# Third place for raw weight words, exponents by PSUM and remainders turned by VectorE, in a top-k attention with an FFN

## The chip, the cores and the metric

The kernel runs on one core of a Trainium2 chip. The metric is the device time of one execution in microseconds (us). Most executions of a kernel agree within 0.3%. A core has five engines with queues of their own: TensorE (PE, its weight loads shown as PEld), VectorE (DVE), ScalarE (ACT), GpSimd (POOL) and SyncE (SP, which only issues DMAs here). [...]

## The reference

Two blocks follow each other: attention that keeps the 32 largest scores of each row, and an FFN without bias.

```python
# q, k, v: (8 batches, 8 heads, 576 rows, 64) fp32
scores = scale * np.matmul(q, k.transpose(0, 1, 3, 2))
kth = np.partition(scores, -32, axis=-1)[..., -32:-31]
scores = np.where(scores >= kth, scores, -1e9)
attn = np.exp(scores - np.max(scores, axis=-1, keepdims=True))
attn = attn / (np.sum(attn, axis=-1, keepdims=True) + 1e-09)
x = heads_to_columns(np.matmul(attn, v))      # 4608 tokens x 512
h = x @ w_in                                  # 512 x 2048
return (h - np.tanh(h)) @ w_out               # 2048 x 512
```

The two weight matrices arrive in 64-bit floating point. The kernel reads their raw words and builds fp32 values itself.

## The kernel before

**Steps.** The attention is cut into 144 steps, 18 for each batch. A step takes a pair of heads (`hp`, four pairs) and 128 query rows of both (`qt`). 576 rows are four tiles of 128 and a remainder of 64; the remainders of two head pairs share one step (`J`, `rem`), two such steps a batch. In `plan()` (L530) the tiles of a batch are grouped into units of two tiles, which share FFN work. In batch 0 the first two tiles are units of one tile; in batch 7 the last two are. The remainders of two batches form a unit of their own (`rest`). A `Unit` has its FFN input `xT`.

**The loop.** The order of all engines is written out by hand (`manual_schedule`). Iteration n of the loop at L683 emits, in this order: `values` of an older step, `mask(n-1)`, `search(n)`, `scores(n+1)`, `expo(n-1)`, and the loads of later steps. `search` (L244) is VectorE's main work: four rounds of MAX8 (L271) and MATCH_REPLACE8 (L274) after two tensor operations on the scores (L263, L264). Between its rounds, `between(i)` places other VectorE work: the transposes of q and k rows (L218), the conversion of weights, and the turning of older weights.

**Turning the softmax weights.** The product with v needs the weights z with keys on partitions. There are two ways. With `pe=True`, `turn_pe` (L389) makes nine TensorE transposes into PSUM (L404) and three ScalarE copies (L407), and `values` follows two iterations after the step (`lag` 2). Otherwise `turn_z` (L365) lets VectorE transpose blocks of 32 x 32 (L372), `spread_keys` (L377) moves the blocks across partitions with 16 DMAs on SyncE's queue (L385), and `values` comes four iterations after the step. Before the change `pe` holds for batch 0, for the one-tile units of batch 7, and for all remainders. `zx2` are the two buffers of the second way, used in turn; the second one and `et_rem`, the turned weights of a remainder, lie in the tile `spare`.

**FFN.** A unit that is complete puts its FFN into the list `work`, in items of equal size: `ffn_h` (L471) computes h in the PSUM tiles `hps` (pool `h_ps`, two buffers) and then h - tanh(h); `ffn_o` (L497) the output product `ops`. `rate()` (L657) chooses how many items a step deals out, in four places of the iteration (`deal`). An item waits until the pieces of the weights that it needs are converted.

**Conversion of weights.** 32 pieces of 128 x 512 (16 of w_in, then 16 of w_out) are converted in iterations 0 to 10, two in each of the first two, three in each of the next eight, four in iteration 10 (`many`, L565). `convert` (L136) is a generator of three parts. It loads the raw words twice (L146, and L147 shifted by three bytes). Part 1 takes the exponent (L156 on VectorE, L157 and L158 on ScalarE) and the mantissa (L160, L163). Part 2 puts the sign to the exponent (L166, VectorE) and multiplies both (L169, GpSimd). `slots` (L128) are the places for raw words: two in `spare`, and one in each quarter of w_out until that quarter's own pieces come. The third entry of a slot is the piece from which it may not be used any more. A slot is loaded again when part 2 has run.

Of the kernel before, what the change touches and what calls it, by code (L numbers as in the profile page):

```python
# [8 lines left out]
AF = mybir.ActivationFunctionType  # L9
ALU = mybir.AluOpType  # L10
# [9 lines left out]
J = 4  # L20
# [28 lines left out]
def kernel(  # L49
# [25 lines left out]
    WJ = 4  # L75
# [34 lines left out]

    NW = 512


    spare = consts.tile([P, 4, NW, 2], U32, name="spare")
    later = spare[:].rearrange("p a n w -> p (a n w)").bitcast(FP32)
    zx2 = [consts.tile([P, 4 * S], FP32, name="zx")[:], later[:, 0 : 4 * S]]
# [8 lines left out]

    slots = [(spare[:, i], spare[:, 2 + i], 8 * CD) for i in range(2)]  # L128
    for j in reversed(range(WJ)):
        halves = [  # L130
            flat(w_out[j][:, 2 * i : 2 * i + 2, :]).bitcast(U32).rearrange("p (n w) -> p n w", w=2)
            for i in range(2)
        ]
        slots.append((*halves, (WJ + j) * CD))

    def convert(piece, slot):  # L136


        j, i = piece // CD, piece % CD
        if j < WJ:  # L140
            src, dst = moe_w_in[i * P : (i + 1) * P, j * NW : (j + 1) * NW], w_in[j][:, i, :]
        else:
            r0 = ((j - WJ) * FJ + i) * P
            src, dst = moe_w_out[r0 : r0 + P, :], w_out[j - WJ][:, i, :]
        raw, shifted, _ = slot
        nc.sync.dma_start(flat(raw), src.bitcast(U32))  # L146
        nc.sync.dma_start(  # L147
            flat(shifted).bitcast(U8)[:, 0 : 8 * NW - 4], src.bitcast(U8)[:, 3 : 8 * NW - 1]
        )
        yield  # L150
        hi = raw[:, :, 1]
        f = thpool.tile([P, NW], FP32, tag="th", name="f")
        fu = f[:].bitcast(U32)


        nc.vector.tensor_scalar(fu, hi, 20, 0x7FF, ALU.logical_shift_right, ALU.bitwise_and)  # L156
        nc.scalar.activation(f[:], fu, AF.Relu, bias=e1151[:], scale=-(2.0**23))  # L157
        nc.scalar.activation(f[:].bitcast(I32), f[:], AF.Relu, bias=e255[:], scale=-1.0)  # L158

        nc.vector.tensor_scalar(  # L160
            dst.bitcast(U32), shifted[:, :, 0], 0x0FFFFFFF, None, ALU.bitwise_and
        )
        nc.scalar.activation(dst, dst.bitcast(U32), AF.Copy, bias=1.0, scale=2.0**-28)  # L163
        yield

        nc.vector.scalar_tensor_tensor(  # L166
            out=fu, in0=hi, scalar=0x80000000, in1=fu, op0=ALU.bitwise_and, op1=ALU.bitwise_or
        )
        nc.gpsimd.tensor_tensor(dst, dst, f[:], ALU.mult)  # L169
        yield  # L170
# [15 lines left out]
    def load_rows(name, b, hp, exact):  # L186

        if b == 0 and hp and not exact:
            x = early[2 * hp - 2 + (name == "q")]
        else:  # L190
            x = ldpool.tile([P, S], FP32, tag=f"{name}in", name=f"{name}in")[:]
        raw[name, b, hp] = x
        src = {"k": k, "q": q}[name]
        for a in range(NG):
            h, d = 2 * hp + a // 2, a % 2 * G
            nc.sync.dma_start(  # L196
                x[a * G : (a + 1) * G, :].rearrange("i (n d) -> i n d", d=G),
                src[b, h, :, d : d + G].rearrange("(n i) d -> i n d", i=G),
            )
# [177 lines left out]
    def spread_keys(n):  # L377


        zx = zxs.pop(n)  # L380
        et = ets[n] = etpool.tile([P, 4 * S], FP32, tag="et", name="et")
        w = steps[n].nq * S // 2
        for a in range(NG):
            for c in range(NG):
                nc.sync.dma_start(  # L385
                    et[group(c), a * w : (a + 1) * w], zx[group(a), c * w : (c + 1) * w]
                )
# [142 lines left out]
    def plan():  # L530
        steps.clear(), done.clear()

        def block(b, qt):
            return [(slice(0, P), out[b * S + qt * P : b * S + (qt + 1) * P, :])]

        rest = None
        for b in range(B):
            if b % 2 == 0:
                rest = Unit(
                    [[(half(i), out[(b + i) * S + JP : (b + i + 1) * S, :]) for i in range(2)]], "xTr"  # L540
                )

            parts = [(0, 1), (2, 3)]
            if b == 0:
                parts[0:1] = [(0,), (1,)]
            if b == B - 1:
                parts[1:2] = [(2,), (3,)]
            for a, qts in enumerate(parts):
                unit = Unit([block(b, qt) for qt in qts], "xT")
                pe = b == 0 or len(qts) == 1  # L550
                for hp in range(NHP):
                    for i, qt in enumerate(qts):
                        steps.append(Step(b, hp, qt, unit, 0, i, len(qts), pe))
                    if hp == NHP - 1:
                        done[len(steps) - 1] = unit
                    if hp % 2 and a == (0 if b == B - 1 else len(parts) - 1):
                        steps.append(Step(b, hp - 1, J, rest, b % 2 * R, pe=True))
                        if hp == NHP - 1 and b % 2:
                            done[len(steps) - 1] = rest
        for g, after in zip(steps, steps[1:]):  # L560
            if after.pe and not after.rem and not g.pe:
                g.lag = 3
# [4 lines left out]
    def run(exact):  # L567
# [4 lines left out]
        def at(n, fn):  # L572
            todo.setdefault(n, []).append(fn)
# [26 lines left out]
        def load_piece():  # L600
            k = len(loaded)
            usable = [x for x in free if x[2] > k]
            if k < pieces and usable:
                free.remove(usable[0])
                piece = convert(k, usable[0])
                next(piece)
                loaded.append((piece, usable[0]))

        def part(x, k):
            next(loaded[k][0])  # L610
# [5 lines left out]
        for _ in slots[NHP:]:  # L616
            at(-4, load_piece)
        started = 0
        for m in range(max(many) + 1 if pieces else 0):
            mine = range(started, min(started + many[m], pieces))  # L620
            started = mine.stop
            seq = [(1, k) for k in mine[:1]]
            for k in mine[1:]:
                seq += [(1, k), (2, k - 1)]
            seq += [(2, k) for k in mine[-1:]]
            for i, x in enumerate(seq):
                at_round.setdefault((m, 3 * i // max(len(seq) - 1, 1)), []).append(
                    lambda x=x: part(*x)
                )
# [27 lines left out]
        def rate():  # L657


            have, low, high = len(work), 0.0, None  # L660
            coming = sorted((t, u.n // 8) for u, t in ready.items() if t > n)
            for t, k in coming + [(NS + 4, 0)]:
                r = have / max(t - n, 1)
                high = r if high is None else min(high, r)
                have += k
            for u, t in begun.items():
                if t > n and u in before:
                    need = [i + 1 for i, x in enumerate(work) if x[1] is before[u]]
                    if need:
                        low = max(low, need[-1] / (t - n))  # L670
            return max(low, high)
# [3 lines left out]
        def deal(part):  # L675
            nonlocal credit
            credit += part * share
            while work and credit > 0 and work[0][0] <= converted[0]:
                work.pop(0)[2]()
                credit -= 1  # L680
            credit = min(credit, 1.0)

        for n in range(-4, NS + 4):  # L683
            pe = here(-2) and steps[n - 2].pe
            if here(-3) and not steps[n - 3].pe:
                spread(n - 3)
            for m in (n - 4, n - 3):
                if 0 <= m < NS and steps[m].last and steps[m].lag == n - m:
                    values(m)
            share = rate()  # L690
            if pe:
                w = turn_pe(n - 2)
                next(w)
            if here(-1):
                mask(n - 1, exact)
            if here(0):
                search(n, exact, between)
            elif here(-2):
                between(0)
            if here(-2) and not pe and steps[n - 2].last:  # L700
                spread_keys(n - 2)
            if pe:
                spread(n - 2)
            deal(0.4)
            if here(1):
                scores(n + 1)
            if pe:
                next(w)
            if here(-1):
                expo(n - 1)  # L710
            deal(0.2)
            if pe and steps[n - 2].last:
                values(n - 2)
            deal(0.2)
            for fn in todo.pop(n, []):
                fn()
            deal(0.2)
# [48 lines left out]
```

## Time and profile before

| | |
|---|---|
| time, 3 runs | 1573.74 us median, 1572.37 to 1576.3 |
| profiled span | 1571.8 us, mean granted TensorE clock 0.977 |
| TensorE busy | 1463.9 us (93%) |
| VectorE busy | 1322.7 us (84%) |
| ScalarE, GpSimd busy | 907.7 and 945.5 us |
| FFN matmuls (L481 and L502) | 476.0 and 524.7 us busy |
| transposes on TensorE (L404) | 360 records, 62.3 us busy |
| conversion L166 | 32 records: 17 with the mean 1165 ns, 15 with 933 ns |
| spread DMAs (L385) | 832 issues |

The page has sums over the span; the 40 slices below it, each 39 us long, show how they are spread. A group of instructions has its busy time, the mean of one in ns, and the idle time of its engine just before it with what ended it. The chain of waits is the sequence of work that ended last, followed back from the end. As matmuls are pipelined and their ends are modelled, TensorE's busy time has to be held against counts of records.

### The profile page before, as it was taken

Reading aid. Unit: us, or ns where it says so; the run is one execution under the profiler, and the core shown is the slowest. Engines: PE = TensorE matmul, PEld = TensorE weight load, DVE = VectorE, ACT = ScalarE, POOL = GpSimd, SP = SyncE. Lnnn points to the kernel's source line nnn. Section 1 sums busy time; section 2 is a strip of 40 time slices with the busy share of each in tenths; the row PEclk is TensorE's granted clock in tenths of the full one; section 3 lists DMA queues with packets and bytes.
Section 4 is the critical chain, followed back from the end, with each engine's and each line's share of the span. In section 5 each row is a group of like instructions: output and inputs, shape, how many; then the busy total and the mean of one; then the engine's idle time right before and its main releaser. Section 6 shows DMA issues by size and latency. Waiting matters only on the chain.

```text
span 1571.8 us, 25605 instructions
## 1 busy us (share of the span) xinstructions
PE 1463.9 (93%) x7834; PEld 940.6 (60%) x7834; DVE 1322.7 (84%) x3810; ACT 907.7 (58%) x1637; POOL 945.5 (60%) x1533
## 2 busy tenths in 40 slices
PE   2566699899999999999999999999999999999998
PEld 1355376556566565656666565656666666666675
DVE  7987689999999999998999999998999899874300
ACT  4877577556556565656556565656555565654431
POOL 2777467657567575657467575756566565644521
PEclk9877799999999999999999999999999999999999
DMA  9844112333532334233432343333432334210000
GB/s 248 297 172 168 69 30 56 88 86 65 115 88 61 90 82 91 69 80 75 100 88 62 84 94 83 74 79 76 97 92 61 82 84 96 55 45 7 8 8 16
DMA packets 245009, 134.43 MB, mean 86 GB/s; under 512 B 205440, under 2 KB 205440, under 8 KB 244864
## 3 DMA queue, kind: packets, MB, share of 16 engines
q1 hardware_dynamic: 244864, 132.71, 34.7%
q8 instruction: 64, 1.05, 0.3%
q14 instruction: 81, 0.66, 0.1%
HBM read 61.85 MB, written 9.44 MB: 45 GB/s over the span
## 4 chain that ended last, share of the span: by engine, by line
PE 81%; DVE 8%; ACT 4%; SPq 3%; POOL 2%; DMA 1%; issue 1%; DVEq 0%; ACTq 0%; POOLq 0%
PE hps L481 29%; PE ops L502 29%; PE av L428 9%; PE scps L233 9%; PE zt L404 2%; DVE m L271 2%; DVE ab L274 2%; PE av L436 2%; SPq L196 1%; SPq L385 1%; DVE f L166 1%; ACT z L303 1%; DMA spare<-in_moe_w_out_dram 1%; ACT sc L241 1%; ACT f L157 1%
## 5 line engine op out<-in xcount | busy, mean ns | idle before, releaser
L502 PE MATMUL ops<-w_out,g 128*128 128x512 f32 x1152 | 524.7, 599 | 0.0
L481 PE MATMUL hps<-xT,w_in 128*128 128x256 f32 (+1 forms) x2304 | 476.0, 362 | 0.2 <-POOL xT L452 0.2
L271 DVE MAX8 m<-ab 128x8 f32<-128x288 f32 (+1 forms) x1152 | 464.9, 445 | 0.0
L306 POOL TENSOR_TENSOR z<-sc,z 128x576 f32<-128x576 f32 x288 | 400.0, 1411 | 106.3 <-ACT z L303 106.3
L481 PEld LDWEIGHTS hps<-xT,w_in 128*128 128x128 f32 x2304 | 399.2, 195 | 63.5 <-issue 14.4
L274 DVE MATCH_REPLACE8 ab<-m,ab 128x288 f32<-128x288 f32 x864 | 376.2, 443 | 0.0
L502 PEld LDWEIGHTS ops<-w_out,g 128*128 128x128 f32 x1152 | 210.9, 192 | 232.0 <-issue 229.7
L303 ACT ACTIVATE z<-sc,tb 128x576 f32<-128x576 f32 x288 | 207.8, 770 | 138.3 <-POOL tb L290 138.3
L495 POOL TENSOR_TENSOR g<-g,th 128x512 f32<-128x512 f32 x144 | 183.8, 1276 | 130.2 <-ACT g L494 126.3
L241 ACT COPY sc<-scps 128x1152 f32<-128x1152 f32 x144 | 160.9, 1117 | 121.5 <-PE scps L233 117.0
L326 ACT ACTIVATE z<-z,nb 128x576 f32<-128x576 f32 x288 | 221.7, 775 | 5.3 <-POOL z L306 5.2
L263 DVE TENSOR_TENSOR ab<-scps,sc 128x576 f32<-128x576 f32 x144 | 107.0, 743 | 133.2 <-POOL bad L310 73.3
L233 PE MATMUL scps<-kT,qT 64*128 64x288 f32 (+1 forms) x1280 | 185.5, 439 | 31.0 <-DVE qT L218 28.8
L233 PEld LDWEIGHTS scps<-kT,qT 64*128 64x128 f32 (+1 forms) x1280 | 100.5, 181 | 122.3 <-issue 65.5
L428 PE MATMUL av<-et,vb 128*64 128x256 f32 (+1 forms) x1152 | 133.5, 368 | 39.9 <-ACT et L407 34.2
L493 ACT ACTIVATE th<-hps 128x512 f32<-128x512 f32 x144 | 85.3, 592 | 114.7 <-PE hps L481 107.1
L452 POOL TENSOR_TENSOR xT<-xs 128x256 f32<-128x256 f32 (+1 forms) x72 | 48.0, 667 | 157.2 <-ACT xs L440 157.0
L428 PEld LDWEIGHTS av<-et,vb 128*64 128x64 f32 x1152 | 77.6, 140 | 100.2 <-ACT et L407 37.8
L440 ACT COPY xs<-av 128x512 f32<-128x512 f32 (+1 forms) x88 | 44.7, 508 | 154.9 <-PE av L436 154.8
L336 POOL TENSOR_SCALAR rd<-den 128x2 f32<-128x2 f32 x144 | 33.4, 232 | 146.7 <-ACT z L326 113.1
L266 DVE MAX8 ab<-ab 128x8 f32<-128x288 f32 x288 | 116.4, 445 | 0.0
L264 DVE TENSOR_TENSOR ab<-scps,sc 128x576 f32<-128x576 f32 x144 | 107.4, 746 | 0.0
(59 smaller groups left out, 1319.0 us busy)
## 6 DMA issues: line engine op xcount, KB each, us to landing
et<-spare SPq DMA_DIRECT2D x416, 72.0 KB, 2.0
et<-zx SPq DMA_DIRECT2D x416, 72.0 KB, 2.0
kin<-in_k_dram SPq DMA_DIRECT2D x116, 72.0 KB, 2.4
qin<-in_q_dram SPq DMA_DIRECT2D x116, 72.0 KB, 2.5
vb<-in_v_dram SPq DMA_DIRECT2D x64, 128.0 KB, 2.5
out_dram<-ot SPq DMA_DIRECT2D x32, 256.0 KB, 2.2
spare<-in_moe_w_out_dram SPq DMA_DIRECT2D x11, 512.0 KB, 4.2
spare<-in_moe_w_out_dram SPq DMA_DIRECT2D x11, 511.5 KB, 5.1
```

Source lines behind the costliest of these rows:

```text
L233: nc.tensor.matmul(ps[rows, t, s, 0:S2], qT[g.b, g.hp + i][half(t), qs], kT[g.b, g.hp + i][half(t), ks], start=True, stop=True,)
L241: nc.scalar.copy(sc[:], ps[:, :, :, 0:S2])
L266: nc.vector.max(ab[:, t, S2 : S2 + 8], lo[:, t, :])
L271: nc.vector.max(m[:, t, m8], last[t] if i == rounds - 1 else cur[t])
L274: nc.vector.match_replace(nxt[t], m[:, t, m8], cur[t], NEG)
L303: nc.scalar.activation(zv[:, t, :], scf[:, t, :], AF.Relu, bias=tb[:, t : t + 1], scale=-BIG)
L306: nc.gpsimd.tensor_tensor(zv[:, t, :], scf[:, t, :], zv[:, t, :], ALU.subtract)
L326: nc.scalar.activation(x["zv"][:, t, :], x["zv"][:, t, :], AF.Exp, bias=x["nb"][:, t : t + 1], scale=scale, accum_out=den[:, t : t + 1],)
L428: nc.tensor.matmul(av[half(t), 0, cols], vb[g.b, hp][:, t, c, :] if c < J else vr[g.b, hp][:, t, :], es[:, :, (J + 1) * t + c if c < J els ...
L481: nc.tensor.matmul(cur[u][:, s : s + w], w_in[j][:, c, fo : fo + P], u.xT[:, c, 0:w], start=(c == 0), stop=(c == CD - 1),)
L495: nc.gpsimd.tensor_tensor(g, g, th[:], ALU.subtract)
L502: nc.tensor.matmul(cur[u][:], u.g[o // 1024][:, o % 1024 // 512, o % 512 : o % 512 + P], w_out[f // FJ][:, f % FJ, :], start=(f == 0), sto ...
```

## The change

It has five parts.

1. A third place for raw words that lasts for all 32 pieces, in the first `zx2` buffer, which no step uses before batch 1. The slot that expires first is now taken first.
2. For the pieces of w_in, the exponent goes from ScalarE to VectorE through a PSUM tile of the pool `h_ps` and no more through SBUF.
3. Three of the four DMAs that load the first q rows are issued on ScalarE's queue. Part 1 of the first piece runs before the first search.
4. Only batch 0 turns its weights by TensorE. The remainders of the batches 1 to 7 and the last two tiles of batch 7 take the second way; these two tiles are one unit again.
5. `deal` counts the pieces that were converted before the iteration began, so that no FFN item is placed ahead of a conversion of the same iteration. In the order of TensorE's instructions nothing moves by this up to step 31.

```diff
+    first = zx2[0][:, 0 : 4 * NW].bitcast(U32).rearrange("p (a n w) -> p a n w", a=2, w=2)
     slots = [(spare[:, i], spare[:, 2 + i], 8 * CD) for i in range(2)]
+    slots.append((first[:, 0], first[:, 1], 8 * CD))
...
-        nc.scalar.activation(f[:].bitcast(I32), f[:], AF.Relu, bias=e255[:], scale=-1.0)
+        e = h_ps.tile([P, NW], FP32, tag="h", name="e")[:] if j < WJ else f[:]
+        nc.scalar.activation(e.bitcast(I32), f[:], AF.Relu, bias=e255[:], scale=-1.0)
...
-            out=fu, in0=hi, scalar=0x80000000, in1=fu, op0=ALU.bitwise_and, op1=ALU.bitwise_or
+            out=fu, in0=hi, scalar=0x80000000, in1=e.bitcast(U32), op0=ALU.bitwise_and, op1=ALU.bitwise_or
...
-            nc.sync.dma_start(
+            queue = nc.scalar if a and (name, b, hp, exact) == ("q", 0, 0, False) else nc.sync
+            queue.dma_start(
...
-        et = ets[n] = etpool.tile([P, 4 * S], FP32, tag="et", name="et")
+        rem = steps[n].rem
+        et = ets[n] = et_rem if rem else etpool.tile([P, 4 * S], FP32, tag="et", name="et")
...
-            if b == B - 1:
-                parts[1:2] = [(2,), (3,)]
...
-                pe = b == 0 or len(qts) == 1
+                pe = b == 0
...
-                        steps.append(Step(b, hp - 1, J, rest, b % 2 * R, pe=True))
+                        steps.append(Step(b, hp - 1, J, rest, b % 2 * R, pe=pe))
...
-                free.remove(usable[0])
-                piece = convert(k, usable[0])
+                slot = min(usable, key=lambda x: x[2])
+                free.remove(slot)
+                piece = convert(k, slot)
...
+        if pieces:
+            at(-1, lambda: part(1, 0))
...
+            seq = [x for x in seq if x != (1, 0)]
...
-            while work and credit > 0 and work[0][0] <= converted[0]:
+            while work and credit > 0 and work[0][0] <= usable:
...
-            share = rate()
+            share, usable = rate(), converted[0]
```

More of the change, by code (lines that the diff above doesn't have):

```diff
@@ L603, in load_piece @@
             if k < pieces and usable:
-                free.remove(usable[0])
-                piece = convert(k, usable[0])
+                slot = min(usable, key=lambda x: x[2])
+                free.remove(slot)
+                piece = convert(k, slot)
                 next(piece)
-                loaded.append((piece, usable[0]))
+                loaded.append((piece, slot))
         def part(x, k):
```

## The prediction

> **What bounds the kernel now.** I read the page's busy line and slices first.
>
> ```profile
> PE 1463.9 (93%) x7834; PEld 940.6 (60%) x7834; DVE 1322.7 (84%) x3810; ACT 907.7 (58%) x1637; POOL 945.5 (60%) x1533
> PE   2566699899999999999999999999999999999998
> DVE  7987689999999999998999999998999899874300
> ```
>
> There are three stages: about 200 us (five slices of 39 us) in which TensorE is half idle, a long middle in which TensorE and VectorE are both full, and a tail from about 1390 us in which VectorE runs out of work. The busy times of each stretch say it in us:
>
> ```profile
> 60.00:80.00 20.00, 8.86 (x47) 6.22 (x48) 19.37 (x50) 16.32 (x32) 15.47 (x20) 0.62 0.67 226
> 160.00:180.00 20.00, 7.35 (x27) 3.36 (x25) 8.45 (x22) 10.80 (x17) 7.20 (x7) 0.76 0.30 105
> 600.00:800.00 200.00, 200.00 (x1023) 124.59 (x1023) 184.19 (x529) 117.26 (x209) 127.70 (x212) 1.00 0.38 84
> ```
>
> (After the length: busy us of PE, PEld, DVE, ACT, POOL, then granted clock, DMA share, GB/s.) A busy PE may be a waiting PE, so I counted. The chain of waits repeats itself from 779.07 to 1129.53 us: 36 steps in 350.5 us. Prices from dense runs: the last unit, and one steady step.
>
> ```profile
> 1536.69 14.29 PE hps L481 x128
> 1550.98 13.75 PE ops L502 x32
> ...
> 711.64 1.04 PE L404 MATMUL zt<-ident,z 128*128 128x128 f32 x8
> 712.40 3.32 PEld L481 LDWEIGHTS hps<-xT,w_in 128*128 128x128 f32 x16
> 712.51 3.62 PE L481 MATMUL hps<-xT,w_in 128*128 128x256 f32 x16
> ```
>
> An hps record of 128 columns takes 14.29/128 = 0.112 us (0.222 at 256), an ops record 13.75/32 = 0.430. One item of the FFN (8 hps records at 256 columns, or 4 ops records) is thus about 1.75 us. The program deals 4 items a step: 144 x 1.75 = 252.0. Scores: 32 x 1.2 + 4 x 2.4 = 48.0. Values of a pair of tiles with rx (from 700.77 to 703.36 in the timeline) 2.6 x 16 = 41.4; of a remainder (719.22 to 720.70) 1.48 x 4 = 5.9. Nine transposes zt of a remainder: the next hps starts 0.87 us after the first eight and about 0.15 us after the ninth, so 1.02 x 4 = 4.1. Sum 351.4 against 350.5: the middle is TensorE work without holes. VectorE, at 92%, is next.
>
> The start is another regime. One VectorE line there has two prices:
>
> ```profile
> 61.79 0.67 DVE L166 SCALAR_TENSOR_TENSOR f<-w_out,f 128x512 uint32<-128x512 uint32 x1
> 62.59 1.27 POOL L169 TENSOR_TENSOR w_in<-w_in,f 128x512 f32<-128x512 f32 x1 [0.92 <-ACT w_in L163]
> 63.13 1.28 DVE L166 SCALAR_TENSOR_TENSOR f<-w_out,f 128x512 uint32<-128x512 uint32 x1
> ...
> 170.44 0.43 DVE L156 TENSOR_SCALAR f<-spare 128x512 uint32<-128x512 uint32 x1 [3.30 <-DMA spare<-in_moe_w_out_dram]
> 176.78 0.43 DVE L156 TENSOR_SCALAR f<-spare 128x512 uint32<-128x512 uint32 x1 [2.55 <-DMA spare<-in_moe_w_out_dram]
> ```
>
> The third line overlaps the POOL product above it and takes twice as long. The last two are VectorE waiting for raw words in step 10, which lasts 27.05 us (L263 at 153.8 to 180.8) where its neighbours last 16 to 17.
>
> [...] L166 takes 0.67 to 0.69 us alone and 1.27 to 1.36 us where a POOL tensor operation runs, while L263 and L264, with one PSUM operand, average 743 and 746 ns. [...] Here the DMA share is 0.98 in the first 20 us, so I expect little.
>
> **The change part by part.**
>
> *First q rows on ScalarE's queue.* The eight issues of the first k and q rows run from 0.72 to 4.90 us, and qT starts at 7.44 when the last row lands. Three issues (1.6 us) go to a queue idle until 10.6 us. Bound: 0 to 1.6; with the DMA engines full I take 0.9. Everything behind on SyncE's queue also moves up, raw words included.
>
> *First half of piece 0 moved before step 0.* L156 and L160 (0.39 + 0.42 us) move into VectorE's idle 3.54 us before L263 at 11.76. Worth 0.8.
>
> *Exponents by PSUM, 16 pieces.* Of the 16 w_in pieces, 9 L166 took 1.27 to 1.35; each falls to 0.68. ScalarE's L158 writes PSUM instead (0.72 us either way, I assume). The two h_ps buffers are free: the first hps comes in step 6, when the last w_in piece is done. In steps 0 to 2 VectorE is full, but the raw words land just in time (piece 3 made L160 wait 0.60 us until 32.32), so I replayed these steps, with the durations of the timeline, against landings 1 us earlier. L263 starts at 10.9 instead of 11.8; VectorE reaches L160 of piece 1 at 16.3 and waits for its words until 17.3 (18.34 before); step 1 starts at 23.0 instead of 23.8. L160 of piece 3 waits until 31.3; step 2 starts at 35.3 instead of 36.8. Pieces 4 to 6 land ahead, the third L166 (1.30 before) saves 0.6 more: step 3 starts at 48.7 to 48.8 instead of 50.9. That is 2.2 us for the three edits together. In steps 3 to 5 (13.4 us each) both long L166 lie on the loop f L158, L166, search, L166, POOL L169, rx, zt, et: 0.67 + 0.61, less about 0.1 where the exponential of L326 ends last: 1.2 a step, 3.6.
>
> *Third place for raw words.* Step 10 loses its waits except for piece 31, requested only when piece 28 is done. Replayed: L166 of piece 28 ends at 165.6 as before, piece 30 follows at once, piece 31 lands about 172, the step ends near 174.7 instead of 180.8: 6.1. Steps 6 to 9 wait for ScalarE and TensorE, not for words: nothing.
>
> Start together: 2.2 + 3.6 + 6.1 = 12. It is kept: steps 11 to 137 get the same number of FFN items as before.
>
> *Remainders of batches 1 to 7 turned by VectorE and DMA.* 14 steps lose 1.02 us of TensorE (and 1.36 of ScalarE, hidden) and gain a 1.36 us transpose on VectorE and 16 DMA issues. In batch 1 VectorE is the limit (no idle time from step 34 to 42); the first remainder's transpose fits into the 2.38 us wait of step 33, the second costs 1.25, so nothing in sum. In batches 2 to 7, 12 x 1.02 = 12.2, if VectorE fits: 92% becomes about 95%. The new wait: `values` of the remainder, at the head of TensorE's order, waits for those DMAs, and all scores and FFN matmuls queue behind it. SyncE's issues take 0.61 us each, 10 us for sixteen; behind the spread of the pair before and eight k and q loads, the remainder's last part lands some 0.5 to 1.5 us before its `values`. I take 2 us lost in all, 0 to 3.5 for each as bounds. So 10.
>
> *Last eight steps.* 8 x 1.02 = 8.2 us of transposes go. Values at 128 columns cost as much as 20 x 0.089 (14 in 1.24 us at 57.46) + 0.15 = 1.92 a step; two make 3.84 against 2.6 for a pair: 4 x 1.24 = 5.0. FFN work is the same 82 items from step 138 on, with 12 more of them behind the last scores; TensorE stays full, since 5 items a step make 11.7 us against VectorE's 9.5. At the end no old FFN work is left between the last values and the last unit's hps: xs and xT, 0.59 + 0.73 + handovers, expose 2.0. Net 11.2.
>
> Sum: 12 + 10 + 11.2 = 33; 1573.7 - 33 = **1540**.
>
> **Rivals.**
> - *Loads gate the start.* The DMA share of 1.08 from 20 to 40 us speaks for it, the free landings from piece 4 on (5 us ahead or more) against. The start gives 1 instead of 12: 1551.
> - *VectorE's gaps come back too.* After each TensorE remainder L263 waits 2.4 to 3.2 us. If that is a true stall, some 1.2 us more for each of 12 goes: 1540 - 14 = 1526. Against it stands the sum of 351.4.
> - *The DMA path is late.* At the upper bound of 3.5 us for every remainder TensorE waits 14 x 3.5 = 49 us on top of the 12 + 12.2 + 11.2 gained: 1574 - 35 + 49 = 1588, slower. For it: two spreads in consecutive steps fill SyncE's queue. Against it: landings of pairs in the trace are 4 us ahead of their use.
>
> **How the numbers follow.** Forecast 0.58, gated start 0.20, returned gaps 0.12, late DMA 0.10, of which 0.06 with a partial loss that still ends at or under 1574 and 0.04 slower. The range, 1526 to 1556, reaches both nearer rivals and leaves out the late DMA. Faster by over 0.3% 0.93 (0.03 of the partial losses end within 0.3%), same 0.03, slower 0.04.
>
> **What would show it.** L166 of the w_in pieces near 0.69 whatever POOL does; step 10 near 21 us; zt gone after batch 0; 36 steps of the middle in 346 to 347 us; a tail of 64 ops records. Wrong if TensorE waits on DMA at the remainder's av, or if VectorE has no idle time in the middle.

## The result and the profile after

The changed kernel takes 1548.53 us (median, 1546.23 to 1550.22) against 1573.05 us for the kernel before on the same chip: a ratio of 0.9839, 95% interval 0.9818 to 0.9861. It was run once more later, on the chip of the last experiments: 1549.55 us against 1574.24, ratio 0.9839 (0.9826 to 0.9853). The gain is 24.5 us; the forecast was 33.

The busy line and the rows of slices of TensorE and VectorE, from the page of the changed kernel:

```profile
PE 1440.6 (93%) x7428; PEld 912.4 (59%) x7428; DVE 1347.3 (87%) x3828; ACT 883.4 (57%) x1567; POOL 941.5 (61%) x1525
PE   2467899999999999999999999999999999999997
DVE  6997889999999999999999999999999999997300
```

406 TensorE records have gone. VectorE is busy 25 us longer and now stays full to the 36th of the 40 slices. The three stretches shown of the kernel before, in the view of busy times by stretch:

```profile
60.00:80.00 20.00, 11.02 (x57) 7.90 (x59) 19.13 (x56) 17.92 (x35) 14.79 (x23) 0.66 0.93 346
160.00:180.00 20.00, 12.53 (x59) 6.31 (x58) 18.23 (x52) 13.98 (x26) 11.03 (x17) 0.74 0.15 53
600.00:800.00 200.00, 199.69 (x991) 127.71 (x990) 190.31 (x541) 118.72 (x210) 131.01 (x214) 1.00 0.41 91
```

From 160 to 180 us VectorE is busy 18.2 us (8.5 before): most of the wait in step 10 is gone. From 600 to 800 us VectorE is at 95%, as forecast, and TensorE has its first holes, 0.3 us in 200.

To see where the time came from, I compared the starts of L267 (L263 before), the first VectorE instruction of every step, up to the last `ops` record. All figures are profiled us; the second column of the changed kernel is its second profile (the experiment `again`).

| stretch | before | after | after, again | gain | forecast |
|---|---|---|---|---|---|
| start to step 3 | 50.9 | 51.0 | 49.1 | -0.1, 1.8 | 2.2 |
| steps 3 to 5 | 40.1 | 37.1 | 37.1 | 3.0 | 3.6 |
| steps 6 to 9 | 62.7 | 60.9 | 61.5 | 1.9, 1.2 | 0 |
| step 10 | 27.1 | 20.6 | 19.7 | 6.5, 7.3 | 6.1 |
| steps 11 and 12 | 16.1 | 17.5 | 17.4 | -1.4, -1.3 | 0 |
| steps 13 to 45, batch 1 for the most part | 299.3 | 301.4 | 302.2 | -2.1, -2.9 | 0 |
| steps 46 to 137 | 895.6 | 887.0 | 887.9 | 8.6, 7.8 | 10 |
| step 138 to the start of the last ops record | 172.3 | 162.1 | 162.1 | 10.2 | 11.2 |
| from there to the end | 7.7 | 10.8 | 10.8 | -3.1 | 0 |
| span | 1571.8 | 1548.3 | 1547.7 | 23.5, 24.1 | 33 |

The groups of the first 100 us show what PSUM did. This is the view of groups by line and shape, for VectorE (count, busy us, mean ns, idle before):

```profile
L169 DVE SCALAR_TENSOR_TENSOR f<-w_out,e 128x512 uint32<-128x512 uint32 x10 | 6.7, 675 | 0.7 <-ACT e L161 0.6
L169 DVE SCALAR_TENSOR_TENSOR f<-w_out,f 128x512 uint32<-128x512 uint32 x2 | 2.1, 1052 | 0.1
L169 DVE SCALAR_TENSOR_TENSOR f<-zx,e 128x512 uint32<-128x512 uint32 x2 | 1.3, 674 | 0.2 <-ACT e L161 0.2
```

In all sixteen pieces with e from PSUM the instruction takes 0.66 to 0.69 us, also in the eight that run under a GpSimd tensor operation from start to end. With f from SBUF, as in the pieces of w_out, the two shown take 1.05 us in the mean; over all sixteen such pieces it is 0.67 to 0.69 us without a GpSimd tensor operation beside it (six) and 1.27 to 1.43 with one (ten). The last lines of the chain of waits:

```profile
1468.94 14.28 issue
1483.26 0.73 POOL xT L457
1484.03 26.60 PE hps L486 x122
1510.63 27.48 PE ops L507 x64
1538.19 0.59 ACT ot L517
```

The tail is the forecast one: one unit of two tiles, 64 ops records, straight behind the last xT.

Two more stages are compared in groups by line and shape, for TensorE. From step 46 to step 137, two lines before and one after:

```profile
L481 PE MATMUL hps<-xTr,w_in 128*128 128x128 f32 x256 | 30.0, 277 | 0.0
L404 PE MATMUL zt<-ident,z 128*128 128x128 f32 x108 | 16.4, 279 | 0.0
L486 PE MATMUL hps<-xTr,w_in 128*128 128x128 f32 x384 | 45.4, 277 | 0.0
```

From step 138 to the last ops record, three lines before and two after:

```profile
L404 PE MATMUL zt<-ident,z 128*128 128x128 f32 x72 | 11.0, 277 | 0.3 <-ACT xs L440 0.3
L428 PE MATMUL av<-et,vb 128*64 128x128 f32 x128 | 8.8, 279 | 0.0
L428 PE MATMUL av<-et,vr 128*64 128x128 f32 x32 | 3.1, 273 | 0.0
L433 PE MATMUL av<-et,vb 128*64 128x256 f32 x80 | 9.7, 385 | 0.0
L433 PE MATMUL av<-et,vr 128*64 128x256 f32 x20 | 3.0, 379 | 0.0
```

All transposes zt are gone from both stages: 108 are nine for each of the twelve remainders of batches 2 to 7, 72 are nine for each of the last eight steps.

### The profile page after: what moved, and what is told of

It is laid out like the page before. It is cut to its first block, busy times and chain, and to the rows that moved or that the text cites. A ratio compares the mean times of both kernels' runs of the same rounds, so it can differ in the third digit from the quotient of the medians.

```text
span 1548.3 us, 25298 instructions
## 1 busy us (share of the span) xinstructions
PE 1440.6 (93%) x7428; PEld 912.4 (59%) x7428; DVE 1347.3 (87%) x3828; ACT 883.4 (57%) x1567; POOL 941.5 (61%) x1525
## 4 chain that ended last, share of the span: by engine, by line
PE 73%; DVE 9%; SPq 5%; ACT 4%; DMA 3%; issue 3%; POOL 2%; DVEq 0%; ACTq 0%; POOLq 0%
PE hps L486 27%; PE ops L507 27%; PE av L433 9%; PE scps L237 8%; SPq L390 4%; DVE ab L278 3%; DVE m L275 3%; PE av L441 2%; SPq L200 1%; DMA zx<-in_moe_w_in_dram 1%; DVE spare L376 1%; DVE ab L270 1%; DVE ab L267 1%; DVE ab L268 1%; ACT sc L245 1%
## 5 line engine op out<-in xcount | busy, mean ns | idle before, releaser
L486 PEld LDWEIGHTS hps<-xT,w_in 128*128 128x128 f32 x2176 | 392.4, 193 | 73.4 <-issue 24.4
L267 DVE TENSOR_TENSOR ab<-scps,sc 128x576 f32<-128x576 f32 x144 | 107.6, 747 | 70.1 <-POOL bad L314 58.2
```

What stands on the lines that cost most here:

```text
L486: nc.tensor.matmul(cur[u][:, s : s + w], w_in[j][:, c, fo : fo + P], u.xT[:, c, 0:w], start=(c == 0), stop=(c == CD - 1),)
```

## The experiments

All times below are medians of four or five runs, with the kernel before at 1573.61, 1572.83 and 1574.24 us in the three groups, each on a chip of its own. Runs of one kernel lie up to 5.0 us apart, so effects of 2 us are read from the traces.

**one_queue.** All first q rows on SyncE's queue.

```diff
-            queue = nc.scalar if a and (name, b, hp, exact) == ("q", 0, 0, False) else nc.sync
+            queue = nc.sync
```

> The changed kernel with all first q rows back on SyncE's queue; the rest as changed. In the changed kernel 10.3 us pass from the last ops record to the end of the span, 3.1 more than in the kernel before, and SyncE's last DRAIN lasts 2.2 us (0.06 before). Theory: the second hardware DMA queue has to be drained at the end; without it the DRAIN is below 0.3 us and the time from the last ops record to the end is 7 to 8 us. The start loses at most 1 us by the later q rows, since the DMA engines are full there. Sum: 1.5 to 2.5 us faster than the changed kernel, about 1546.5. Rival A: the end has nothing to do with the queue (another length of the last stores); DRAIN stays at 2.2 us, the time is 1548.5 to 1550. Rival B: the two queues are worth 2 us at the start; then 1550 or more even if the end gets shorter.

Measured: 1551.07 us, ratio 0.9855 (0.9840 to 0.9870). The theory fell. The pause at the end stays, 2.2 us, only at another instruction of SyncE's list: it now lies three instructions earlier, at a semaphore wait and not at the DRAIN, just as many as the three issues that were put into the list. The last ops record starts 10.7 us before the end, as before this edit. And in this one profile the second queue is worth more than I thought. Step 0 starts at 12.5 us, in the kernels with two queues at 10.3 to 11.2. Part of this is the new place of part 1 of piece 0: VectorE stands at its L163 for the second copy until 12.15 us, while ScalarE's copy of the scores, for which the first search waits, has ended at 11.31. What was to save 0.8 us delays the first search by 1.2 us here, and by 0.5 in `rem1_pe`, the latest of the starts with two queues. From the timeline of VectorE in this kernel:

```profile
33.39 0.43 DVE L157 TENSOR_SCALAR f<-w_out 128x512 uint32<-128x512 uint32 x1 [0.94 <-DMA w_out<-in_moe_w_in_dram]
34.67 0.43 DVE L163 TENSOR_SCALAR w_in<-w_out 128x512 uint32<-128x512 uint32 x1 [0.85 <-DMA w_out<-in_moe_w_in_dram]
```

This is piece 3, for which VectorE waits twice; its second copy lands at 34.65 us, at 30.75 to 33.59 in the eleven profiles with two queues and all loads.

**no_psum.** The exponents of w_in through SBUF again.

```diff
-        e = h_ps.tile([P, NW], FP32, tag="h", name="e")[:] if j < WJ else f[:]
+        e = f[:]
```

> The changed kernel with the exponents of w_in through SBUF again. Theory: steps 3 to 7 gained 4.7 us by PSUM (3.0 in steps 3 to 5, 1.7 in steps 6 and 7); they come back, L169 of VectorE takes 1.27 to 1.36 us again where a POOL product runs, and steps 3 to 5 last 13.3 to 13.4 us. Steps 0 to 2 wait for raw words, so they lose at most 0.5. Time about 1553 (4.5 to 5 us more than 1548.5). Rival: the gain of steps 3 to 7 came from the third place for raw words or from the FFN items held back by the new test in deal; then the time stays within 1 us of 1548.5 and steps 3 to 5 at 12.2 to 12.7. Second rival: only steps 3 to 5 come back and 6 and 7 do not: 1551.5.

Measured: 1554.05 us, ratio 0.9873 (0.9858 to 0.9888). Steps 3 to 6 take 13.4 us each again, 3.5 us more in sum; step 13 starts 3.7 and 5.8 us later than in the two profiles of the changed kernel. The groups of the first 100 us, VectorE:

```profile
L169 DVE SCALAR_TENSOR_TENSOR f<-w_out,f 128x512 uint32<-128x512 uint32 x11 | 11.3, 1028 | 1.9 <-ACT f L161 1.9
L169 DVE SCALAR_TENSOR_TENSOR f<-zx,f 128x512 uint32<-128x512 uint32 x2 | 2.6, 1317 | 0.6 <-ACT f L161 0.6
```

The gain of steps 3 to 6 is that of PSUM. It also works in the steps before: step 3 starts 18.6 us after the second copy of piece 3 has landed, as in the kernel before, and 17.4 us after it with PSUM, 1.3 us less. Here the place of the exponents alone was changed, SBUF for PSUM: 675 ns became 1028, and 674 became 1317 (means; a third group, with the words in `spare`, went from 669 to 828). The gain of step 7 does not belong to it: this step took 14.6 us in the first profile of the changed kernel and 16.1 in its second.

**old_places** and **late_first.** The change took part 1 of piece 0 out of step 0, and by this the other parts moved up one place in the search. In `old_places` they stay where they were:

```diff
-            seq = [x for x in seq if x != (1, 0)]
             for i, x in enumerate(seq):
+                if x == (1, 0):
+                    continue
```

> The changed kernel, with the conversion parts of step 0 in the places of the search where they were before the change (part 1 of piece 1 after the second round and no longer after the first). Theory A: by taking part 1 of piece 0 out of step 0, the change moved part 1 of piece 1 forward to the first place, where VectorE meets raw words that have not landed (waits of 0.59 and 1.84 us before its two instructions); one round of MAX8 and MATCH_REPLACE8, about 2.4 us, ahead of it hides these waits. Step 0 falls from 13.3 to about 11.3 us. Of this 1.3 to 2 us are kept: 1546.5 to 1547. Theory B (loads gate the start whatever the order): step 1 waits so much longer for piece 3, which still lands at 33.6; step 0 is 2 us shorter, step 1 2 us longer, and the time stays at 1548.5.

In `late_first` steps 0 and 1 also convert one piece after the other:

```diff
+            if m < 2:
+                a, b = mine
+                seq = [(1, a), (2, a), (1, b), (2, b)]
```

> The changed kernel, with steps 0 and 1 converting one piece after the other: part 2 of the first piece comes before part 1 of the second, so part 1 of piece 1 and of piece 3 sits in the third place of the search. Theory A (place, not load): both steps lose their waits for raw words (2.4 us in step 0, 1.8 in step 1), steps 0 and 1 last 11 and 12 us, and 3 to 4 us are kept: 1545. Theory B (loads gate): piece 3 lands at 33.6, VectorE reaches it at about 33, so nothing is left to wait for in step 1, but steps 2 and 3 then wait for pieces 4 and 5; time 1548. Third possibility: the later part 2 of pieces 1 and 3 delays the POOL product and what is behind it in step 1 and 2; 1549 to 1550.

Measured: 1548.87 us (0.9841, 0.9828 to 0.9855) and 1550.33 (0.9852, 0.9837 to 0.9867). In `old_places` step 0 falls to 10.7 us, as theory A says, and step 1 rises to 15.1, as theory B says. From its timeline of VectorE:

```profile
31.20 0.43 DVE L157 TENSOR_SCALAR f<-w_out 128x512 uint32<-128x512 uint32 x1 [2.36 <-DMA w_out<-in_moe_w_in_dram]
32.48 0.43 DVE L163 TENSOR_SCALAR w_in<-w_out 128x512 uint32<-128x512 uint32 x1 [0.85 <-DMA w_out<-in_moe_w_in_dram]
```

What step 0 saves, VectorE waits for piece 3. Step 3 starts 17.4 us after the second copy of piece 3 has landed; it is 17.4 in every kernel with PSUM and these pieces in steps 0 to 2, whatever the order inside step 0. In `late_first` it is 17.9, so the later part 2 costs some 0.5 us. Theory B holds for both.

**light_loads.** Less data in the first 35 us: the second copy of pieces 0 to 3 is not loaded.

```diff
-        nc.sync.dma_start(
-            flat(shifted).bitcast(U8)[:, 0 : 8 * NW - 4], src.bitcast(U8)[:, 3 : 8 * NW - 1]
-        )
+        if piece < 4:
+            shifted = raw
+        else:
+            nc.sync.dma_start(
+                flat(shifted).bitcast(U8)[:, 0 : 8 * NW - 4], src.bitcast(U8)[:, 3 : 8 * NW - 1]
+            )
```

> The changed kernel in which the second, shifted copy of the raw words of pieces 0 to 3 is not loaded (their mantissas are taken from the first copy, so these four pieces of w_in are wrong); 2.1 MB less before step 3. Theory: the DMA engines are full in the first 35 us and the landings of pieces 0 to 3 gate steps 0 to 2. Without these bytes step 0 starts at 10 or before, no wait for raw words is left in steps 0 to 2, they last about 10.7, 12 and 13 us, and step 3 starts at 46 to 47 instead of 51.0. The time is 3 to 5 us shorter, 1544 to 1545. Rival: VectorE's own work and the chain over ScalarE and GpSimd set these steps; step 3 starts at 49 or later and the time is 1547 to 1549.

Measured: 1546.06 us, ratio 0.9826 (0.9812 to 0.9839). No wait for raw words is left after step 0 has begun; steps 0 and 1 last 10.7 and 11.7 us, and step 3 starts at 46.8. So the loads gate steps 0 and 1. But not much of it is kept: step 7 takes 17.1 us, and step 13 starts at 183.8, only 1.1 us ahead of the second profile of the changed kernel.

**no_third.** Without the third lasting place.

```diff
-    slots.append((first[:, 0], first[:, 1], 8 * CD))
```

> The changed kernel without the third lasting place for raw words (the choice of the place that expires first stays). Theory: step 10 waits again for words requested too late, 26 to 27 us instead of 20.6; VectorE waits for DMA before the exponents of pieces 29 and 30. One fewer piece is loaded ahead, so the first steps may get their words 1 us earlier. Time 1553 to 1555. Rival: the choice of the place alone is enough (the w_out quarters are used up first and the two lasting places are kept for the end); then step 10 stays near 21 us and the time at 1548 to 1549.

In this kernel piece 23 lies in a quarter of w_out whose first own piece is begun before piece 23 is finished, so that its sign words are overwritten; the instructions are the same. Measured: 1557.32 us, ratio 0.9901 (0.9886 to 0.9916). Its profile is that of its shortest run, with a span of 1553.7 us. In it step 10 takes 25.7 us, 5.2 to 6.0 more than with the third place. From the timeline of VectorE:

```profile
164.38 0.43 DVE L156 TENSOR_SCALAR f<-spare 128x512 uint32<-128x512 uint32 x1 [3.10 <-DMA spare<-in_moe_w_out_dram]
165.55 0.43 DVE L162 TENSOR_SCALAR w_out<-spare 128x512 uint32<-128x512 uint32 x1 [0.74 <-DMA spare<-in_moe_w_out_dram]
170.35 0.43 DVE L156 TENSOR_SCALAR f<-spare 128x512 uint32<-128x512 uint32 x1 [2.20 <-DMA spare<-in_moe_w_out_dram]
171.52 0.43 DVE L162 TENSOR_SCALAR w_out<-spare 128x512 uint32<-128x512 uint32 x1 [0.74 <-DMA spare<-in_moe_w_out_dram]
```

The changed kernel has in this step:

```profile
165.41 0.43 DVE L157 TENSOR_SCALAR f<-spare 128x512 uint32<-128x512 uint32 x1 [0.28 <-DMA spare<-in_moe_w_out_dram]
166.58 0.43 DVE L163 TENSOR_SCALAR w_out<-spare 128x512 uint32<-128x512 uint32 x1 [0.74 <-DMA spare<-in_moe_w_out_dram]
```

The waits of 3.10 and 2.20 us are for the most part what the third place takes away; the choice of the place alone does not do it. That the median lies above the profile's run is not followed up.

**rem_pe** and **rem1_pe.** The remainders on TensorE again, those of all batches and those of batches 0 and 1 alone.

```diff
-                        steps.append(Step(b, hp - 1, J, rest, b % 2 * R, pe=pe))
+                        steps.append(Step(b, hp - 1, J, rest, b % 2 * R, pe=True))
```

In `rem1_pe` the last argument is `pe=b < 2`.

> The changed kernel with the remainders of batches 1 to 7 turned by TensorE again (two iterations after the step); the last two tiles of batch 7 stay a pair turned by VectorE. Theory: the remainders gave 8.9 us in batches 2 to 7 and about 2 in batch 7's last steps, and cost about 2 in batch 1, where VectorE has no idle time; so the time goes up by 8 to 9 us to 1557, batch 1 alone gets 2 us shorter, and 36 steps of the middle take 350.5 us again instead of 347.3. Rival A: TensorE takes the transposes back without loss because VectorE, at 95%, had become the limit; then at most 3 us more, 1549 to 1551. Rival B: with the remainders back on TensorE the waits of 2.4 to 3.2 us of VectorE cost extra; more than 12 us, above 1560.

> The changed kernel with the remainders of batch 1 alone turned by TensorE again. Theory: VectorE is the limit in batch 1 and the two transposes cost 2.2 us there (steps 13 to 46 take 301.4 us in the changed kernel, 299.3 before and with all remainders on TensorE); 2.2 us come back. Besides, 32 DMAs and their waits leave SyncE's list, so that its end does not reach instruction 1945, at which seven kernels paused for 1.9 to 2.2 us; the time from the last ops to the end falls from 10.8 to 8.2 to 8.5 us. Sum 4.5 us: 1544. Rival A: the pause depends on time, not on the place in the list, and stays: 1546. Rival B: the lead of batch 1 is lost later, in the middle, since TensorE gets 2 us more work: 1548.

Measured: 1553.08 us (0.9876, 0.9861 to 0.9891) and 1547.88 (0.9828, 0.9815 to 0.9842).

`rem_pe`: steps 46 to 137 take 895.6 us, the time before the change; so the 7.8 to 8.6 us of this stage are the remainders' and nothing else's. Steps 13 to 45 take 299.2, also the time before. The last stretch to the ops record takes 162.3 us, 0.3 more than in the changed kernel. The 2 us that I expected of batch 7's remainders there were a misreading of the plan: these are steps 130 and 135, and the 108 zt records shown above put their transposes into the stage before. From step 13 to 137 this kernel has the times and the TensorE records of the kernel before; so the fifth part of the change moves no FFN work there, and the last eight steps alone gain 10.0 us (172.3 less 162.3).

`rem1_pe`: steps 13 to 45 take 299.2 us, 2.2 and 2.9 less than with VectorE. The reason is not the one that I wrote. TensorE's waits between 340 and 490 us, in the view of waits, for the changed kernel:

```profile
PE av L433 <- DMA spare<-spare: 2.0, 1, 2.0
PE av L433 <- DMA et<-spare: 1.0, 1, 1.0
PE av L433 <- DMA qin<-in_q_dram: 0.2, 1, 0.2
PE hps L486 <- POOL xT L457: 0.2, 1, 0.2
```

In `rem1_pe` the same view is empty. These are the late DMAs of the third rival. The first is the remainder's own; the second is that of a pair of tiles, whose sixteen issues stand on SyncE's queue behind those of the other remainder. VectorE's own account is near the forecast: from step 30 to 45 it is busy 2.6 us longer than in `rem1_pe`, but the wait of 2.4 us in step 33 is gone. New are waits of 0.8 to 1.0 us in step 34 and 0.4 to 1.4 in step 41, which `rem1_pe` does not have. In the second profile of the changed kernel the sixteen issues of the first remainder run from 361.5 to 372.3 us on SyncE's queue, the last part lands at 374.3, and `av` starts at 374.5 after a wait of 1.8.

**tail_pe.** The last two tiles of batch 7 as two units, turned by TensorE.

```diff
+            if b == B - 1:
+                parts[1:2] = [(2,), (3,)]
...
-                pe = b == 0
+                pe = b == 0 or len(qts) == 1
```

> The changed kernel with the last two tiles of batch 7 as two one-tile units turned by TensorE again; all remainders of batches 1 to 7 stay with VectorE. Theory: of the 10.2 us that the changed kernel gained from step 138 on, the transposes (8 x 1.02) and the values at 128 columns (4 x 1.24) made 13.2, less what is now exposed before the last unit's hps; all but 0.5 of it comes back, and the time goes up by 10 to 12 us to about 1559. Rival: the last steps are short of other work for TensorE, so that the transposes ran in holes; then 5 us or less, 1552 to 1553.

Measured: 1557.75 us, ratio 0.9898 (0.9883 to 0.9913). From step 138 to the last ops record it takes 174.1 us, 12.1 more than with the pair. TensorE is 97% busy in the stretch from 1373 to 1463 us, and what it is idle there is one wait, so there are no other holes for the transposes. The view of busy times, and that of TensorE's waits from 1373 us on:

```profile
1373.00:1463.00 90.00, 87.33 (x503) 60.14 (x502) 38.66 (x127) 40.31 (x79) 38.61 (x63) 1.00 0.05 15
PE av L433 <- DMA spare<-zx: 2.6, 1, 2.6
```

This wait is for the spread of the last remainder, whose values here come three iterations after the step and not four; the changed kernel has waits of 0.4 us in all in this stretch. So 2.2 of the 12.1 us come from the wait and some 10 from the units of one tile. From the last ops record to the end it takes 8.2 us and not 10.8, which hides 2.6 of the 12.1. The rival with holes falls.

**again, later_pieces, both.** The changed kernel as a baseline; one piece less in step 1 and the last two in step 11; and this together with `rem1_pe`.

```diff
-    many = {0: 2, 1: 2, 10: 4} | {n: 3 for n in range(2, 10)}
+    many = {0: 2, 1: 1, 11: 2} | {n: 3 for n in range(2, 11)}
```

> The changed kernel once more, as the baseline on the same chip for the three others. In the kernels so far that share their code up to step 2, the second copy of piece 3 landed between 30.75 and 33.59 us (33.59 in the changed kernel's first profile), and step 3 started 17.35 to 17.4 us after it. Theory (the landing gates the start and varies from execution to execution): the same distance here, and a landing somewhere from 30.5 to 33.6; the time is 1546 to 1549 with it. Rival (the late landing belongs to this kernel): 33.4 to 33.7 again, step 3 at 51.0.

> The changed kernel with one piece instead of two in step 1, three instead of four in step 10 and the last two in step 11 (steps 2 to 10 take three each, from piece 3 on). Theory (the landing of piece 3 gates step 1): step 1 has no wait for it and takes about 11.5 us, step 2 gets three pieces whose words have landed; step 10 lasts about 17.5 and step 11 about 12 us; step 13 starts 1 to 3 us earlier, the time is 1546 to 1547.5. Rival: the work is only moved, and step 11 waits for the last pieces as step 10 did; step 13 at 184 to 187 as in the kernels so far, 1548.5. Second rival: FFN items of steps 6 to 11 wait longer for their weights and TensorE lacks work there; 1550.

> The last two edits together. Theory: they act in different stages and add up: about 1542 to 1543, 1.5 us or more less than rem1_pe alone. Rival: what the start gains is lost before step 46, where VectorE has no idle time and its order is fixed; then the time of rem1_pe, 1544.

Measured: 1549.55 us (0.9839, 0.9826 to 0.9853), 1551.48 (0.9852, 0.9839 to 0.9865) and 1546.44 (0.9828, 0.9814 to 0.9842). In `again` the second copy of piece 3 lands at 31.77 us and step 3 starts 17.4 us later: the landing varies from execution to execution, by almost 3 us.

In `later_pieces` step 1 takes 10.5 us, step 3 starts at 45.9 and step 11 at 160.5, against 167.4 in `again`. At step 13 nothing of it is left: 185.3 against 184.9. VectorE's waits from 160 to 190 us:

```profile
DVE ab L267 <- ACT sc L245: 4.3, 1, 4.3
```

and TensorE's in the same stretch:

```profile
PE zt L409 <- ACT z L330: 4.8, 1, 4.8
PE av L433 <- ACT et L412: 2.4, 1, 2.4
PE av L441 <- POOL rx L355: 1.9, 1, 1.9
```

In `again` VectorE waits 1.5 and 0.7 us for its L267 in this stretch, and TensorE 7.1 us at zt and nowhere else. The work was only moved: VectorE now waits for scores in one place. That the later pieces delay the chain over ScalarE and TensorE fits these waits, but was not tested by itself. `both` has the gain of `rem1_pe` in steps 13 to 45 (299.3 us) and the lowest median, 3.1 us under the baseline of its group; its interval overlaps that of the changed kernel. No version is shown to beat the changed kernel by its time; that turning batch 1's remainders on TensorE is worth 2 to 3 us in its stage is shown by two traces.

## Why the prediction was right or wrong

The direction holds, and so do the three mechanisms that the forecast rests on: the exponents read from SBUF (1028 ns in `no_psum`, 675 from PSUM), the words requested too late (5.2 to 6.0 us in step 10), and TensorE's transposes (12.5 us for 108 records). Of the 33 us forecast, 9 are missing, and where a stage came out near its figure, part of that is luck. For the two dense stages, the time from the start of each TensorE record to the start of the next was added up by tile, with waits over 0.15 us apart; the prices of records below are from these sums.

*Start, 12 forecast, 9.9 and 12.0 measured.* The third place (6.1) is confirmed by `no_third` (5.2 to 6.0). PSUM (3.6 in steps 3 to 5) gave 3.0 there and 0.4 in step 6; `no_psum` takes both back. The 2.2 us of steps 0 to 2 rest on landings 1 us earlier, and that step failed. PSUM's part came, 1.3 us less between the landing of piece 3 and step 3. But the second copy of piece 3, at 32.30 us before, lands between 30.75 and 33.59, so the gain there is between -0.1 and 2.8 us from one execution to the next. My bound for the second queue was too low at its likeliest value: 0.9 us, my estimate from 1.6 us of issues and a DMA share of 0.98, where `one_queue` has a landing 1.1 to 3.9 us later. The first rival, gated loads, is right for steps 0 and 1, but it does not reach step 10. That the second profile meets the 12 is luck: steps 6 to 9 gained 1.2 to 1.9 us and step 10 0.4 to 1.2 more than forecast, and steps 11 and 12 lost 1.3 to 1.4. Beyond the 0.4 of step 6 this was not taken apart; in the profiles with the same pieces in these steps, step 7 varies by 2.5 us.

*Batch 1, 0 forecast, -2.1 and -2.9 measured.* The step that failed is "so nothing in sum": I counted VectorE's 1.36 us and put the 2 us for late DMAs into batches 2 to 7. The late DMAs are there, 3.0 us of wait in the changed kernel, but in batch 1. The third rival is right in kind, then, and far from its bound of 49 us.

*Batches 2 to 7, 10 forecast, 8.6 and 7.8 measured.* `rem_pe` gives the whole of it back. The 12.2 us for the transposes is right: the 108 zt records take 12.5 us before. TensorE's waits are 0.7 and 1.6 us, less than the 2 put in. What failed is the assumption behind "the same number of FFN items": the number is the same (368), but the FFN matmuls take 3.2 and 3.0 us longer in this stage, and 12.5 less these and the waits is the measured gain. Nearly half of the 3.2 is the mixture at the ends of the stage: the values of the remainders come later, so it has the hps of three units of remainders and not of two (the x384 and x256 above), in place of 26 ops records and 9 hps of 256 columns. The rest is that records take a little longer, an hps of 256 columns 0.2246 us instead of 0.2234; why, is open (in `rem1_pe`, with two such units, FFN matmuls still take 2.7 us longer). The second rival, the returned gaps of VectorE, fell: 36 steps take 347.3 to 347.9 us, just above the 346 to 347 that I wrote.

*Last eight steps, 11.2 forecast, 10.2 measured.* This is near for the wrong reasons. The transposes are right, 8.4 us for 72 records where I had 8.2. The 5.0 for values at 128 columns failed: with their rx they take 0.9 us more than at 256. I had priced a record of 128 columns at 0.089 us, from 14 records in the 1.24 us from 57.46 on. This stretch begins with four slow ones and reaches to the end of the last, 0.27 us of its own; in between, two records start every 0.11 us. In the tail a record takes 0.062. The exposure before the last unit's hps was too large at 2.0: TensorE waits 0.4 us in the whole stretch, 0.3 before. And FFN matmuls of 1.2 us have gone from this stretch, which I did not foresee. The errors of 4.1 too much and of 1.9 and 1.2 too little cancel for the most part.

*The end, not forecast, -3.1.* I took the end of the program as fixed. The last store takes 4.2 us to land instead of 3.3, and then SyncE's list pauses for 2.2 us. I first laid this to the second DMA queue, and `one_queue` refuted it. Then I laid it to a place in SyncE's list, and `rem1_pe` refuted that: its list is 39 instructions shorter, and the pause is still there, now on GpSimd, whose DRAIN comes 2.0 us after SyncE's. The kernels with 1611, 1688 and 1871 instructions executed by SyncE do not show it (7.7, 8.5 and 8.2 us from the last ops record to the end); those with 1910 to 1952 do (10.0 to 10.9). The program ends with a branch over the exact repetition, and the pause comes 15 to 18 instructions after it on SyncE. In the eight kernels whose SyncE pauses, it comes ahead of the same instruction by count, number 1945 from 0 (in the changed kernel the DRAIN at 1547.09 us, behind one at 1544.90), which also gives the shift by three in `one_queue`; in the three whose SyncE executes too few to reach it, GpSimd pauses. But the three kernels without the pause end with the same branch, and no run here varies the branch or the count by itself, so the cause stays open.

## What to carry to other kernels

When an edit takes work out of an engine's list, look at what moves into its place, and ask what the engine then meets: in steps 0 and 1 the saved time was only changed into a wait for the same load (2.36 us ahead of piece 3 in `old_places`, 0.91 in the changed kernel). Cost a new DMA path batch by batch, with the issues of the queue counted against the instruction that needs the last one, since two late landings in batch 1 made TensorE wait 3 us, as much as the transposes of three remainders had taken. Take the price of pipelined instructions from start to start in a full stretch (the 384 hps records above last 277 ns each in the mean and keep TensorE busy for 45.4 us, 0.118 each): from the first start to the last end of a short burst, 0.062 us became 0.089. And compare stage by stage with two profiles of the same kernel, because a stage gated by loads, with the DMA engines at a share of 1.0, varied by 3 us, as much as several of the effects sought.

## What was unexpected in the hardware

The first loads gained about as much from a second queue as the time of the issues that went to it: with 1.6 us of issues moved, step 0 starts 1.3 to 2.2 us earlier than in the one profile of `one_queue`. It counts here because the first search waits for these transfers: VectorE's transpose of q stood 1.74 us for them in the kernel before, 0 and 0.48 us in the two profiles of the changed one. The other surprise is the pause of 1.9 to 2.6 us at the end, which appears and vanishes with edits that have nothing to do with the end.
